# A gated mix of windowed attention and SwiGLU: how the first tokens, the identity and the warm-up are started

## The chip, the cores and the metric

The kernel runs on one core of one Trainium2 chip. The metric is the device time of one execution in microseconds (us); the figure for a kernel is the median of several runs. The core has five engines that run side by side, each with its own instruction stream: TensorE (PE: matrix products and transposes; its weight loads, PEld, overlap the products), VectorE (DVE), ScalarE (ACT), GpSimd (POOL) and SyncE (SP, which here only issues transfers). Transfers between memory and the on-chip buffers are issued by SyncE, ScalarE and GpSimd. Engines wait for each other and for transfers by semaphores.

## What is computed

```python
x = A_x                                    # 1 x 2048 x 512, bf16
g = _sigmoid((x * gate_w).sum(-1, keepdims=True))
a = _A_ref(x, A_wqkv, A_wo)                # attention: 32 heads of 16, causal, window of 256, output projection
b = _B_ref(x, B_w1, B_w3, B_w2)            # SwiGLU: (silu(x @ w1) * (x @ w3)) @ w2, inner width 1376
return g * a + (1 - g) * b
```

Every product contracts over the 512 features, so the kernel needs x with features on the partitions. The first 512 tokens are loaded as they lie and transposed on TensorE with an identity matrix; the later tokens come in through transposing transfers.

## The kernel before

All loads are issued at the start, most of them on SyncE's queue:

```python
def x_dma(t, h):                           # 256 tokens
    xs = xp.tile([P, 2, D], BF16, name=f"xs{h}")[:]
    nc.sync.dma_start(
        out=xs,
        in_=x2d[512 * t + 256 * h:512 * t + 256 * (h + 1), :].rearrange("(m p) d -> p m d", p=P))
    xs_tiles[2 * t + h] = xs

def x_dma1(j):                             # 128 tokens: j = 0 on SyncE's queue, j = 1 on ScalarE's
    if j == 0:
        xs_tiles[0] = xp.tile([P, 2, D], BF16, name="xs0")[:]
    (nc.scalar if j else nc.sync).dma_start(out=xs_tiles[0][:, j, :], in_=x2d[j * P:(j + 1) * P, :])
# [...]
nc.scalar.activation(out=scr[:, 1:2], in_=scr[:, 0:1], func=ACT.Tanh)
dma("x00", "SP", 3.5, lambda: x_dma1(0))                                 # tokens 0 to 127
dma("x01", "SP", 3.6, lambda: x_dma1(1))                                 # tokens 128 to 255
dma("x1", "SP", 4.5, lambda: x_dma(0, 1))                                # tokens 256 to 511
dma("k0", "ACT", 4.8, lambda: w_dma(nc.scalar, wk_sb, A_wqkv, 0, P, D))  # key weights, 128 columns
dma("q0", "SP", 5.8, lambda: w_dma(nc.sync, wq_sb, A_wqkv, 0, P))        # query weights, 128 columns
# [... more key and query weights, value weights, later tokens, feed-forward weights ...]
```

The numbers are the landing times that the kernel's own list scheduler assumes. This scheduler runs while the program is built: it gives every engine a fixed order of instructions, which doesn't depend on anything at run time.

GpSimd makes the identity (`ident`), the mask that separates even from odd heads (`eo`), columns of ones in the value tiles (they make the softmax denominators) and the triangular masks (`keep`), and issues the load of the gate vector:

```python
nc.gpsimd.memset(ident[:], 0.0)
nc.gpsimd.affine_select(out=ident[:], in_=ident[:], pattern=[[-1, P]],
                        compare_op=ALU.not_equal, fill=1.0, base=0, channel_multiplier=1)
nc.gpsimd.memset(eo[:], 1.0)
# [... two selects on eo, two operations on VectorE ...]
nc.gpsimd.memset(Vn[:, :, DH:2 * VW:DH + 1], 1.0)      # line 191
nc.gpsimd.memset(Vn[:, :, 2 * VW:], 1.0)
nc.gpsimd.memset(Vs[:, :, VW:], 1.0)
# [... keep: two memsets, four selects ...]
gate_dma()                                             # 128 x 512, broadcast, on GpSimd's queue
```

In the compiled program GpSimd's order is: fill of `ident`, fill of `eo`, the long fill of `Vn`, and only then the select that finishes `ident`.

TensorE begins with six products of constants that nobody reads (the warm-up), in the PSUM bank that the first transposes take next:

```python
b = ps.tile([P, 512], F32, name="g0")
for i in range(NWARM):                                 # NWARM = 6
    nc.tensor.matmul(b[:], lhsT=nc.const_aps.tensor(1.0, (P, P), BF16),
                     rhs=nc.const_aps.tensor(1.0, (P, 512), BF16), start=(i == 0), stop=(i == NWARM - 1))
```

Then come sixteen transposes of 128 x 128 in four groups (the groups `g_151` and `g_156` from tokens 0 to 255, `g_162` and `g_168` from tokens 256 to 511), their copies to `xT` on ScalarE and VectorE, and the first projections, keys (`g_176`, which needs the key weights) and queries (`g_182`), in halves of 256 tokens:

```python
for c in range(NDC):                                   # group of 128 tokens, `half` is 0 or 1
    nc.tensor.transpose(out=tx[:, c, :], in_=xs_tiles[0][:, half, c * P:(c + 1) * P], identity=ident[:])
# [...]
nc.tensor.matmul(b[:, 0:n], lhsT=(wq_sb if is_q else wk_sb)[:, dc, c * P:(c + 1) * P],
                 rhs=xT[:, dc, t0:t1], start=(dc == 0), stop=(dc == NDC - 1))
```

At the end, each tile of 128 tokens is written out from VectorE's result, for tiles 0 to 5 in two halves:

```python
for i in range(0, n, n // (2 if m < 6 else 1)):
    j = i + n // (2 if m < 6 else 1)
    nc.sync.dma_start(out=out2d[m * P:(m + 1) * P, n0 + i:n0 + j], in_=ot[:, i:j])
```

Of the kernel before, what the change touches and what calls it, by code (L numbers as in the profile page):

```python
# [9 lines left out]
BF16 = mybir.dt.bfloat16  # L10
# [3 lines left out]
DH = 16  # L14
WIN = 256
P = 128
# [3 lines left out]
VW = NPAIR * (DH + 1)  # L20

@with_exitstack
def kernel(
# [12 lines left out]
    nc = tc.nc  # L36
    x2d = A_x.flatten_outer_dims()
    out2d = out.flatten_outer_dims()
    S, D = x2d.shape
# [14 lines left out]
    Vn = pp.tile([P, NT, 2 * VW + DH], BF16, name="Vn")  # L54
    Vs = pp.tile([P, NT, VW + DH], BF16, name="Vs")
# [36 lines left out]
    def hold(pool, key, n):  # L92

        refs[(pool, key)] = n
# [10 lines left out]
    xs_tiles = {}  # L105

    def x_dma(t, h):
        xs = xp.tile([P, 2, D], BF16, name=f"xs{h}")[:]
        nc.sync.dma_start(
            out=xs,  # L110
            in_=x2d[512 * t + 256 * h:512 * t + 256 * (h + 1), :].rearrange("(m p) d -> p m d", p=P))
        xs_tiles[2 * t + h] = xs

    def x_dma1(j):
        if j == 0:
            xs_tiles[0] = xp.tile([P, 2, D], BF16, name="xs0")[:]
        (nc.scalar if j else nc.sync).dma_start(out=xs_tiles[0][:, j, :], in_=x2d[j * P:(j + 1) * P, :])

    def xt_dma(t, c):
        nc.sync.dma_start_transpose(out=xT[:, c, 512 * t:512 * (t + 1)],  # L120
# [10 lines left out]
    def dma(name, eng, at, fn):  # L131

        fn()
        land[name] = at

    nc.scalar.activation(out=scr[:, 1:2], in_=scr[:, 0:1], func=ACT.Tanh)
    dma("x00", "SP", 3.5, lambda: x_dma1(0))
    dma("x01", "SP", 3.6, lambda: x_dma1(1))
    dma("x1", "SP", 4.5, lambda: x_dma(0, 1))
    dma("k0", "ACT", 4.8, lambda: w_dma(nc.scalar, wk_sb, A_wqkv, 0, P, D))  # L140
    dma("q0", "SP", 5.8, lambda: w_dma(nc.sync, wq_sb, A_wqkv, 0, P))
# [15 lines left out]
                          in_=B_w2[0:(NFC - 1) * P, :].rearrange("(f p) n -> p f n", p=P)),  # L157
# [7 lines left out]
    def gate_dma():  # L165
        nc.gpsimd.dma_start(out=gw, in_=gate_w.rearrange("(x d) -> x d", x=1).to_broadcast([P, D]))

    def xn_dma():
        nc.sync.dma_start(out=xm[:], in_=x2d[S // 4:S // 2, :].rearrange("(m p) d -> p m d", p=P))
        nc.sync.dma_start(out=xn, in_=x2d[S // 2:S, :].rearrange("(m p) d -> p m d", p=P))  # L170

    def wo_dma():
        for j in range(2):
            wo_t.append(xp.tile([P, 2, D], BF16, name=f"xs{j}"))
            nc.sync.dma_start(out=wo_t[j][:], in_=A_wo[256 * j:256 * (j + 1), :].rearrange(
                "(c p) n -> p c n", p=P))
# [11 lines left out]
    nc.vector.tensor_reduce(out=maskEO[:, 0, 0, :], in_=eo[:], axis=mybir.AxisListType.X, op=ALU.add)  # L188
    nc.vector.tensor_scalar(out=maskEO[:, 0, 1, :], in0=maskEO[:, 0, 0, :], scalar1=-1.0, scalar2=1.0,
                            op0=ALU.mult, op1=ALU.add)  # L190
    nc.gpsimd.memset(Vn[:, :, DH:2 * VW:DH + 1], 1.0)
    nc.gpsimd.memset(Vn[:, :, 2 * VW:], 1.0)
    nc.gpsimd.memset(Vs[:, :, VW:], 1.0)

    keep = []
    for far in (False, True):
# [5 lines left out]
                                    base=-1 if far else 0, channel_multiplier=1 if far else -1)  # L202
        keep.append(k)
    gate_dma()

    class Load:
        def __init__(self, at):
# [6 lines left out]
    def pe_unit(dur, parts, deps, acq=(), rel=(), kind="", more=None):  # L214


        prev = None
        n = len(parts)
        more = more or [[]] * n
        for j, fn in enumerate(parts):  # L220
            o = Op("PE", dur / n, fn, deps + more[j] if j == 0 else [prev] + more[j], acq=acq if j == 0 else (),
                   rel=rel if j == n - 1 else (), kind=kind)
            o.cont = j > 0
            o.head = head = o if j == 0 else head
            prev = o
        return head, prev

    def bank(key, dtype=F32, shape=(P, 512)):
        n = slot("g", key)
        g_tile[key] = ps.tile(list(shape), dtype, name=f"g{n}")  # L230
        return g_tile[key]
# [367 lines left out]
    def add_out(m, n0=0, n1=512):  # L599
        key = ("o", m, n0)  # L600
        hold("g", key, 1)
        n = n1 - n0

        def pe(c0):
            def fn():
                b = bank(key) if c0 == 0 else g_tile[key]
                for c in range(c0, c0 + 1):
                    nc.tensor.matmul(b[:, 0:n], lhsT=OT[:, c * S + m * P:c * S + (m + 1) * P],  # L608
                                     rhs=wo_t[c // 2][:, c % 2, n0:n1], start=(c == 0),
                                     stop=(c == NDC - 1))  # L610
            return fn

        def fin(eng):
            ot = smpool.tile([P, D], BF16, name="ot")
            nc.vector.scalar_tensor_tensor(out=ot[:, 0:n], in0=g_tile[key][:, 0:n],
                                           scalar=gq[:, m:m + 1], in1=bsb[:, m, n0:n1],
                                           op0=ALU.mult, op1=ALU.add)
            for i in range(0, n, n // (2 if m < 6 else 1)):
                j = i + n // (2 if m < 6 else 1)
                nc.sync.dma_start(out=out2d[m * P:(m + 1) * P, n0 + i:n0 + j], in_=ot[:, i:j])  # L620

        a0, a = pe_unit(0.87 * n / 512, [pe(i) for i in range(NDC)], [pv_out[(c, m)] for c in range(NDC)] + [loads["wo"], down_pe[m]],
                        acq=[("g", key)], kind="out")
        Op("DVE", 0.05 + 0.65 * n / 512, fin, [a, down_op[m]], rel=[("g", key)], rank=0.2)
        return a0
# [203 lines left out]
    T0, PACE, NWARM = 11.2, 2.59, 6  # L829
# [200 lines left out]
    with tc.manual_schedule():  # L1030
        b = ps.tile([P, 512], F32, name="g0")
        for i in range(NWARM):
            nc.tensor.matmul(b[:], lhsT=nc.const_aps.tensor(1.0, (P, P), BF16),  # L1033
                             rhs=nc.const_aps.tensor(1.0, (P, 512), BF16), start=(i == 0), stop=(i == NWARM - 1))
        done = set()
        for o in order:
            if not wo_t and o in burst_ops[7:] and done.issuperset(z_op[0:4]):
                wo_dma()
                xn_dma()
            done.add(o)  # L1040
            if o.eng == "PE":
                o.fn()
            else:
                o.fn(o.eng)
# [27 lines left out]
```

The softmax here doesn't subtract the row's maximum and nothing guards it: scores larger than these inputs give would overflow.

## Time and profile before

| What | Value |
|---|---|
| median of three runs | 230.66 us (230.55 to 232.02) |
| the profiled run | 230.98 us, span of the core 229.3 us |
| PE / DVE / ACT / POOL busy | 225.5 / 180.6 / 175.5 / 175.3 us |
| long fill of `Vn` (line 191) | 0.98 to 3.25 us |
| first transpose on PE | 3.71 us |
| first projection on PE (`g_176`) | 5.38 us |
| last product ends | 226.49 us |

The profile is a record of one execution. Its summary gives the busy time of each engine as a share of the span; the chain of waits goes back from the last instruction to whatever released it; the timeline lists instructions by their start; the list of transfers gives the time from issue to landing. "PEld" is the weight load of TensorE. A name such as `g_151` is a PSUM tile, `xs_89` holds tokens 0 to 255, `xs_92` tokens 256 to 511, `on` is the identity and `OT` takes the gate vector in the beginning. Names such as `L191` are lines of the program. The granted clock that the profile lists is 1.00 in every stretch, also in the first microseconds, where the spacing of the products shows half the later rate.

### The profile page before, as it was taken

How to read it: one execution, taken by the hardware profiler on the slowest of the kernel's cores; microseconds unless marked ns; L12 is line 12 of the kernel's file. 1: busy time of each engine (PE TensorE's matmuls, PEld its weight loads, DVE VectorE, ACT ScalarE, POOL GpSimd, SP SyncE). 2: the span in 40 equal slices, each digit the busy share in tenths (PEclk: the TensorE clock that was granted, in tenths of full speed). 3: DMA queues.
4: the chain of work that ended last, by engine and by line, in shares of the span. 5: the costliest groups of instructions: out<-in, count | busy, mean ns of one | idle time of the engine just before them, and what ended most of it. 6: DMA issues, size and time to landing. Idle time of an engine off the chain costs nothing.

```text
span 229.3 us, 7274 instructions
## 1 busy us (share of the span) xinstructions
PE 225.5 (98%) x3060; PEld 102.1 (45%) x3060; DVE 180.6 (79%) x315; ACT 175.5 (77%) x144; POOL 175.3 (76%) x395
## 2 busy tenths in 40 slices
PE   8999999999999999999999999999999999999995
PEld 4543433535344443544353435444443444354544
DVE  2768599999998997879758596949987688876754
ACT  3478889788989989787989897987899877977030
POOL 8048898888899898888878887877888878777200
PEclk9999999999999999999999999999999999999999
DMA  6999999401100000000000000000000001220202
GB/s 187 214 265 202 319 258 350 132 0 26 27 3 3 3 0 0 3 4 4 0 3 0 3 3 3 0 3 4 0 3 1 3 4 37 70 82 0 94 3 93
DMA packets 20337, 13.81 MB, mean 60 GB/s; under 512 B 9680, under 2 KB 20016, under 8 KB 20304
## 3 DMA queue, kind: packets, MB, share of 16 engines
q1 hardware_dynamic: 19056, 11.80, 18.3%
q0 software_dynamic: 432, 1.25, 3.4%
q8 instruction: 24, 0.39, 0.7%
q10 hardware_dynamic: 816, 0.30, 0.5%
q14 instruction: 9, 0.07, 0.1%
HBM read 8.55 MB, written 2.10 MB: 46 GB/s over the span
## 4 chain that ended last, share of the span: by engine, by line
PE 97%; POOL 1%; issue 0%; DVE 0%; POOLq 0%
PE big L710 11%; PE g_1928 L578 1%; PE g_3349 L578 1%; PE g_2556 L578 1%; PE g_2293 L578 1%; PE g_3614 L578 1%; PE g_1297 L578 1%; PE g_4322 L578 1%; PE g_4387 L578 1%; PE g_3016 L578 1%; PE g_3813 L578 1%; PE g_2168 L578 1%; PE g_4282 L578 1%; PE g_2755 L578 1%; PE g_1650 L578 1%; PE g_4503 L578 1%
## 5 line engine op out<-in xcount | busy, mean ns | idle before, releaser
L480 PEld LDWEIGHTS <-w_sb 128*128 128x128 bf16 x320 | 29.2, 98 | 35.3 <-issue 3.4
L784 PEld LDWEIGHTS <-Vn 64*32 64x32 bf16 x720 | 15.1, 91 | 2.9 <-issue 1.3
L784 PEld LDWEIGHTS <-Vs 64*32 64x32 bf16 x720 | 15.2, 91 | 0.2
L809 DVE STREAM_TRANSPOSE OT<-on 128x512 bf16<-128x512 bf16 x16 | 11.2, 703 | 0.1
L339 PEld LDWEIGHTS <-wk_sb 128*128 128x128 bf16 x68 | 6.2, 100 | 7.1 <-issue 1.5
L386 PEld LDWEIGHTS <-xT 128*128 128x128 bf16 x64 | 5.7, 98 | 7.4 <-issue 1.6
L339 PEld LDWEIGHTS <-wq_sb 128*128 128x128 bf16 x68 | 6.0, 98 | 6.7 <-issue 1.5
L410 POOL DMA_DIRECT2D Vs<-Vn x4 | 2.5, 616 | 8.2 <-DVE xs_92 L422 8.2
L608 PEld LDWEIGHTS <-OT 128*128 128x128 bf16 x60 | 5.6, 98 | 6.8 <-issue 0.2
L578 PEld LDWEIGHTS <-hT_680 128*128 128x128 bf16 (+1 forms) x44 | 4.0, 98 | 5.1 <-issue 0.8
L578 PEld LDWEIGHTS <-hT_2291 128*128 128x128 bf16 (+1 forms) x44 | 4.0, 98 | 5.0 <-issue 0.6
L422 DVE SCALAR_TENSOR_TENSOR OT<-OT 128x512 bf16<-128x512 bf16 x8 | 5.9, 757 | 0.0
L578 PEld LDWEIGHTS <-hT_345 128*128 128x128 bf16 (+1 forms) x44 | 3.9, 98 | 4.3
L584 ACT ACTIVATE bsb<-g_4387,omg 128x512 bf16<-128x512 f32 x1 | 0.7, 687 | 6.2 <-PE g_4387 L578 6.2
L578 PEld LDWEIGHTS <-hT_3272 128*128 128x128 bf16 (+1 forms) x33 | 3.1, 98 | 3.8 <-issue 0.2
L734 POOL TENSOR_SCALAR_AFFINE_SELECT e_1530<-e_1530 64x256 bf16<-64x256 bf16 x6 | 3.7, 611 | 0.3
L734 POOL TENSOR_SCALAR_AFFINE_SELECT e_1261<-e_1261 64x256 bf16<-64x256 bf16 x6 | 3.6, 596 | 0.3
L734 POOL TENSOR_SCALAR_AFFINE_SELECT e_976<-e_976 64x256 bf16<-64x256 bf16 x6 | 3.2, 528 | 0.6 <-ACT e_976 L718 0.3
L1033 PE MATMUL g_144<-const-bfloat16-1.0 128*128 128x512 bf16 x6 | 2.7, 623 | 0.8 <-PEq L1056 0.8
L734 POOL TENSOR_SCALAR_AFFINE_SELECT e_423<-e_423 64x256 bf16<-64x256 bf16 x6 | 3.3, 542 | 0.3
L734 POOL TENSOR_SCALAR_AFFINE_SELECT e_3832<-e_3832 64x256 bf16<-64x256 bf16 x6 | 2.5, 411 | 1.1 <-ACT e_3832 L718 0.8
L734 POOL TENSOR_SCALAR_AFFINE_SELECT e_2774<-e_2774 64x256 bf16<-64x256 bf16 x6 | 2.5, 411 | 1.1 <-ACT e_2774 L718 0.8
(928 smaller groups left out, 853.9 us busy)
## 6 DMA issues: line engine op xcount, KB each, us to landing
w_sb<-in_B_w_dram SPq DMA_DIRECT2D x2, 864.0 KB, 8.0
w_sb<-in_B_w_dram SPq DMA_DIRECT2D x1, 1280.0 KB, 8.2
out_dram<-ot SPq DMA_DIRECT2D x9, 128.0 KB, 1.9
Vs<-Vn POOLq DMA_DIRECT2D x8, 136.0 KB, 4.1
w_sb<-in_B_w_dram SPq DMA_DIRECT2D x2, 512.0 KB, 4.9
OT<-in_A_x_dram SPq DMA_DIRECT2D x1, 1024.0 KB, 10.8
out_dram<-ot SPq DMA_DIRECT2D x13, 64.0 KB, 1.6
e_87<-in_A_wqkv_dram SPq DMA_DIRECT2D x1, 512.0 KB, 5.1
```

The costliest lines, as they stand in the source:

```text
L339: nc.tensor.matmul(b[:, 0:n], lhsT=(wq_sb if is_q else wk_sb)[:, dc, c * P:(c + 1) * P], rhs=xT[:, dc, t0:t1], start=(dc == 0), stop=(dc = ...
L386: nc.tensor.matmul(b[:], lhsT=xT[:, c, m * P:(m + 1) * P], rhs=wv_sb[:, c, :], start=(c == 0), stop=(c == NDC - 1))
L410: nc.gpsimd.dma_start(out=Vs[0:HK, ms, 0:VW], in_=Vn[HK:P, ms, 0:VW])
L422: nc.vector.scalar_tensor_tensor(out=x, in0=x, scalar=1.0, in1=gw, op0=ALU.mult, op1=ALU.mult, accum_out=zt[:, m:m + 1])
L480: nc.tensor.matmul(b[:], lhsT=wsb[:, dc, f * P:(f + 1) * P], rhs=xT[:, dc, t * 512:(t + 1) * 512], start=(dc == 0), stop=(dc == NDC - 1))
L578: nc.tensor.matmul(b[:], lhsT=h_tile[t][0:fs, f, (m % 4) * P:(m % 4 + 1) * P], rhs=w2_sb[0:fs, f, :], start=(f == 0), stop=(f == NFC - 1))
L608: nc.tensor.matmul(b[:, 0:n], lhsT=OT[:, c * S + m * P:c * S + (m + 1) * P], rhs=wo_t[c // 2][:, c % 2, n0:n1], start=(c == 0), stop=(c == ...
L710: nc.tensor.matmul(big[:, u, col:col + q1 - q0], lhsT=kt[32 * u:32 * u + 32, (j % 8) * P:(j % 8 + 1) * P], rhs=qt[32 * u:32 * u + 32, q0 - ...
L734: nc.gpsimd.affine_select(out=tri, in_=tri, pattern=[[0, 4], [-1 if far else 1, HK]], compare_op=ALU.is_ge, fill=0.0, base=-1 if far else ...
L784: nc.tensor.matmul(pv[i][32 * u:32 * u + 32, a - qa:b - qa], lhsT=v_of(j, i, 4 * c + u), rhs=e_tile[k][i * HK:i * HK + HK, u, col:col + b ...
L809: nc.vector.transpose(out=OT[:, c * S + qa:c * S + qb], in_=st["on"][:, 0:nb].rearrange("p b i d -> p (b i d)"))
L1033: nc.tensor.matmul(b[:], lhsT=nc.const_aps.tensor(1.0, (P, P), BF16), rhs=nc.const_aps.tensor(1.0, (P, 512), BF16), start=(i == 0), stop=( ...
```

## The change

The change is meant to let the first transposes start earlier. Tokens 0 to 127 are cut into two half rows of 256 features, one on each hardware queue. Tokens 128 to 255 move to SyncE's queue, tokens 256 to 511 to ScalarE's, ahead of the key weights there. On GpSimd the ones in the value tiles come last, after the identity, the masks and the gate's load. The warm-up products get 480 columns instead of 512. One output tile (tile 5) is written in one piece instead of two. The order of instructions on TensorE and VectorE, and that of ScalarE's computations, stay as they were.

```diff
@@ x_dma, x_dma1
-        nc.sync.dma_start(
+        nc.scalar.dma_start(
             out=xs,
             in_=x2d[512 * t + 256 * h:512 * t + 256 * (h + 1), :].rearrange("(m p) d -> p m d", p=P))
@@
-        (nc.scalar if j else nc.sync).dma_start(out=xs_tiles[0][:, j, :], in_=x2d[j * P:(j + 1) * P, :])
+            nc.scalar.dma_start(out=xs_tiles[0][:, 0, D // 2:D], in_=x2d[0:P, D // 2:D])
+            nc.sync.dma_start(out=xs_tiles[0][:, 0, 0:D // 2], in_=x2d[0:P, 0:D // 2])
+        else:
+            nc.sync.dma_start(out=xs_tiles[0][:, 1, :], in_=x2d[P:2 * P, :])
@@ the scheduler's assumed landing times
-    dma("x00", "SP", 3.5, lambda: x_dma1(0))
-    dma("x01", "SP", 3.6, lambda: x_dma1(1))
+    dma("x00", "SP", 3.3, lambda: x_dma1(0))
+    dma("x01", "SP", 3.7, lambda: x_dma1(1))
@@ GpSimd
-    nc.gpsimd.memset(Vn[:, :, DH:2 * VW:DH + 1], 1.0)
-    nc.gpsimd.memset(Vn[:, :, 2 * VW:], 1.0)
-    nc.gpsimd.memset(Vs[:, :, VW:], 1.0)
 # [... keep masks ...]
     gate_dma()
+    nc.gpsimd.memset(Vn[:, :, DH:2 * VW:DH + 1], 1.0)
+    nc.gpsimd.memset(Vn[:, :, 2 * VW:], 1.0)
+    nc.gpsimd.memset(Vs[:, :, VW:], 1.0)
@@ output
-            for i in range(0, n, n // (2 if m < 6 else 1)):
-                j = i + n // (2 if m < 6 else 1)
+            for i in range(0, n, n // (2 if m < 5 else 1)):
+                j = i + n // (2 if m < 5 else 1)
@@ warm-up
-            nc.tensor.matmul(b[:], lhsT=nc.const_aps.tensor(1.0, (P, P), BF16),
-                             rhs=nc.const_aps.tensor(1.0, (P, 512), BF16), start=(i == 0), stop=(i == NWARM - 1))
+            nc.tensor.matmul(b[:, 0:480], lhsT=nc.const_aps.tensor(1.0, (P, P), BF16),
+                             rhs=nc.const_aps.tensor(1.0, (P, 480), BF16), start=(i == 0), stop=(i == NWARM - 1))
```

## The prediction

> **What bounds the kernel now.** I read four views in this order: the summary of engines, the chain that ended last, the timeline of the first microseconds, and the list of transfers with their times to landing. The first two say where a change could count at all.
>
> ```profile
> PE 225.5 (98%) x3060; PEld 102.1 (45%) x3060; DVE 180.6 (79%) x315; ACT 175.5 (77%) x144; POOL 175.3 (76%) x395
> PE 97%; POOL 1%; issue 0%; DVE 0%; POOLq 0%
> ```
>
> The matrix engine is busy 98% of the span and makes 97% of the chain. The stretches of the span show it busy for all but about 0.03 us between 3.7 and 226.5 us. So what starts later than 3.7 us moves the end only if it makes this engine wait, and time can be saved only in the first 3.7 us, plus at the very end (2.8 us), which the change leaves alone. The chain, in order of time, names what fills that start:
>
> ```profile
> 0.95 0.10 POOL eo L183
> 1.05 2.22 POOL Vn L191
> 3.27 0.07 issue
> 3.33 0.30 POOL on L181
> 3.64 0.08 issue
> 3.71 0.58 PE g_151 L246 x4
> ...
> 5.58 0.66 PE g_176 L339 x4
> 6.24 0.44 PE g_182 L339 x4
> ```
>
> Columns are start, length, what. GpSimd fills the value tile with ones for 2.22 us (line 191) before it can finish the identity (line 181), at 3.63; the first transposes begin at 3.71. But the chain names only the last of several arrivals. The timeline and the transfers give the other two:
>
> ```profile
> 0.85 2.72 PE L1033 MATMUL g_144<-const-bfloat16-1.0 128*128 128x512 bf16 x6 [0.85 <-PEq L1056]
> 3.68 0.77 PEld L246 LDWEIGHTS <-xs_89 128*128 128x128 bf16 x8 [1.03 <-DMA xs_89<-in_A_x_dram]
> xs_89<-in_A_x_dram SPq DMA_DIRECT2D x1, 128.0 KB, 2.7
> xs_92<-in_A_x_dram SPq DMA_DIRECT2D x1, 256.0 KB, 3.1
> wk_sb<-in_A_wqkv_dram ACTq DMA_DIRECT2D x1, 128.0 KB, 3.5
> OT<-in_gate_w_dram POOLq DMA_DIRECT2D x1, 128.0 KB, 5.0
> ```
>
> The warm-up matmuls end at 0.85 + 2.72 = 3.57; the first transpose waits for them too, because it takes the same PSUM bank (its queue shows a semaphore wait that ends at 3.6). The first 128 tokens were issued at 0.81 and landed 2.7 later, at 3.51. So three things end within 0.12 us: tokens 3.51, warm-up 3.57, identity 3.63. **Taking away any one of them alone gains next to nothing**; the change touches all three.
>
> [...] four groups of 128 columns take 0.43 us (transposes up to 5.58), while 4 x 256 columns take 0.44 from 6.24 on, twice the rate; the group between, 0.66, holds the step, near 5.8. [...] In the trace the rate is 348 to 357 GB/s between 2.4 and 3.2 us, where 1 KB pieces move, and 287 between 4.0 and 4.8, where 256 B pieces do. [...]
>
> **The change part by part.**
> 1. *Identity first.* What stands before it then are four short fills: they overlap, and in the trace start about 0.1 apart, so that the last ends near 1.2. With 0.07 of wait and 0.29 for the select, the identity is ready near 1.6 instead of 3.63. It stops mattering. The fills of ones end later, near 6.8 (keep masks 2 x 0.55, the gate's issue 0.69, then 2.27 + 0.31 + 0.30), but the first value write starts at 10.18: hidden.
> 2. *Narrower warm-up.* Six matmuls lose 32 columns each. Weight loads start 0.427 apart for 512 columns, so 0.83 ns a column: 6 x 32 x 0.83 = 0.16 us. The end moves from 3.57 to 3.41.
> 3. *Two half rows.* Before, the first 128 KB shared the engines with the next 128 KB, issued at the same moment on the other queue, so 256 KB had to move for either to be done. Now both queues carry the first 128 KB. At 350 GB/s the 128 KB left out are 0.37 us. As the first 0.4 us of traffic is slow (166 GB/s) and half rows are small, I take 0.15 to 0.35: landing at 3.15 to 3.35.
>
> So the start is now set by the warm-up: 3.41 plus the same 0.14 from its end to the first transpose, 3.55 instead of 3.71. **The start gains 0.16 us, not the 2 us of the fill.**
> 4. *What comes behind.* Tokens 128 to 255 are issued at about 1.26 instead of 0.81 and have to be there at 3.71 + 0.43 - 0.16 = 3.98. 384 KB must have moved by then; before, this many had moved by about 3.4 (traffic summed over 0.2 us windows), so with some 0.45 from the last packet to the landing (tokens 256 to 511: last packets near 3.95, landed at 4.36), 3.85: just in time. Tokens 256 to 511 are issued at the same 1.26, now on ScalarE's queue; before they landed at 1.26 + 3.1 = 4.36 against a use at 4.42. The use is now at 4.26. The key weights no longer share the engines with them; the query weights do, 0.4 later. Estimate 4.15 to 4.35: up to 0.1 of wait.
> 5. *Key weights.* They were second on ScalarE's queue (issued 1.30, landed 4.8) and are now third (near 1.73), behind 256 KB. By their end 768 KB of tokens, key and query weights have moved, where before it was some 690 (summed in the same way to 4.4 us, where their last packets are); at 287 GB/s that is 0.28 us later, and what the next weights on SyncE's queue take adds up to 0.3. Landing 5.1 to 5.4; the use at 5.30 moves to 5.14. Expected wait 0.1.
> 6. *Output in one piece for tile 5.* One issue of 0.37 us less on SyncE's queue, near 200 us. No engine waits for it: 0.
>
> Sum: 0.16 gained, about 0.1 given back at the keys, 0.06 left. If the clock still steps up at 5.8, what moved ahead of it ran at half rate and is worth half: 0.03. If nothing has to wait, 0.16. So 0.03 to 0.16, around 0.1.
>
> **The rivals.**
> *The key weights become the wait.* For: five transfers in a row before them on two queues, and small pieces. Against: before they had 0.5 us of slack. If they land at 5.6, the first projection starts 0.3 later than before and the whole is 0.1 to 0.3 slower, near 230.9.
> *The gate vector disturbs.* Its transfer of 128 KB now leaves GpSimd near 3.2 instead of 4.54, so its packets come near 5.5 to 7 instead of 7 to 8.8, amid the value weights. They would delay these by 0.37; they landed at 3.32 + 5.1 = 8.4 and the first use is at 9.12. Against an effect: slack of 0.7, of which the earlier start takes 0.16. Worth 0.
> *The tokens set the start after all.* If half rows land no earlier than 3.51, the start is about 3.65, a gain of 0.06 or less, 230.6.
> *The clock step moves.* [...] each microsecond of half rate costs half a microsecond. The three times before, 230.55 to 232.02, spread by 1.5 us, much more than the whole effect. For: nothing else in a chain of 97% matrix work varies so easily. It makes the comparison uncertain, not the mean.
>
> **Range and chances.** The median of 230.66 less 0.1 is 230.56; as the change trims all three arrivals and some waits may turn out shorter than I sized them, I put 230.5. The range has to hold the spread between runs more than the effect: 229.9 to 231.2. 2% would be 4.6 us, more than the whole start of 3.7 us, so faster by that much is out of reach, and a slowdown of this size would need a wait of which I see no sign: 0.01 each way, 0.98 within.
>
> **What would show it.** In the changed kernel's profile: the ones-fill leaves the chain, and the warm-up or a transfer takes its place; identity done near 1.6; warm-up end near 3.41; first transpose at 3.5 to 3.6; the first weight load of the keys near 5.2, with an idle gap of about 0.1 ahead of it, ended by the transfer of key weights; the step of rate near 5.8; from there the same spacing as before, down to the end. I am wrong if the first transpose starts before 3.4 (the warm-up isn't the floor), if the keys start later than 5.4, or if the end moves by much more or less than the matrix engine's first warm group does.

## The result and the profile after

The changed kernel takes **232.25 us** (median of six runs, 231.67 to 233.34) against 230.75 us for the kernel before (six runs, 230.55 to 232.02). The ratio is 1.0064, 95% interval 1.0034 to 1.0093: 1.5 us slower, within 2%, and outside the predicted range of 229.9 to 231.2. The two profiled executions took 231.67 and 230.98 us, with spans of 230.0 and 229.3.

The summary of engines and the chain by engine of the changed kernel, which answer to the first two lines shown of before:

```profile
PE 225.8 (98%) x3060; PEld 102.0 (44%) x3060; DVE 180.8 (79%) x315; ACT 175.4 (76%) x144; POOL 174.6 (76%) x395
PE 93%; DMA 3%; ACT 1%; SPq 1%; POOL 0%; issue 0%; DVE 0%
```

The work of the matrix engine is the same. But 3% of the chain, which before was 97% matrix work, is now one transfer. The chain in order of time says which:

```profile
2.69 0.04 issue
2.73 0.51 SPq L127
3.24 0.04 issue
3.29 6.33 DMA e_87<-in_A_wqkv_dram
9.62 0.05 issue
9.66 1.04 PE g_215 L389 x4
```

Columns are start, length, what. `e_87` holds the value weights, 512 KB. They are issued at 3.29, land at 9.62, and the first value product starts 0.04 later. Before, it started at 9.12 and waited for no transfer. The lines of the timeline before, for the gate's load, the keys and the values:

```profile
4.54 0.69 POOL L166 DMA_DIRECT2D OT<-in_gate_w_dram  x1
5.38 0.87 PE L339 MATMUL g_176<-xT,wk_sb 128*128 128x256 bf16 x4
9.12 1.03 PE L386 MATMUL g_214<-e_87,xT 128*128 128x512 bf16 x4
```

The timeline of the changed kernel's first ten microseconds shows that what was meant to happen at the start did happen, and where the time went:

```profile
0.84 2.56 PE L1036 MATMUL g_145<-const-bfloat16-1.0 128*128 128x480 bf16 x6 [0.84 <-PEq L1059]
1.29 0.29 POOL L184 TENSOR_SCALAR_AFFINE_SELECT on<-on 128x128 bf16<-128x128 bf16 x1
2.92 0.69 POOL L169 DMA_DIRECT2D OT<-in_gate_w_dram  x1
3.52 0.77 PEld L249 LDWEIGHTS <-xs_89 128*128 128x128 bf16 x8 [0.97 <-DMA xs_89<-in_A_x_dram]
3.55 0.58 PE L249 MATMUL g_152<-on,xs_89 128*128 128x128 bf16 x4
4.45 0.77 PEld L264 LDWEIGHTS <-xs_93 128*128 128x128 bf16 x8 [0.15 <-DMA xs_93<-in_A_x_dram]
5.38 0.56 PEld L342 LDWEIGHTS <-wk_sb 128*128 128x128 bf16 x4 [0.16 <-DMA wk_sb<-in_A_wqkv_dram]
8.24 0.59 PEld L342 LDWEIGHTS <-wq_sb 128*128 128x128 bf16 x4 [0.28 <-DMA wq_sb<-in_A_wqkv_dram]
9.66 1.04 PE L389 MATMUL g_215<-e_87,xT 128*128 128x512 bf16 x4 [0.34 <-DMA e_87<-in_A_wqkv_dram]
```

Brackets hold the idle time before an instruction and what ended it. The identity is ready at 1.58 and the transposes start at 3.55, 0.16 earlier. At the keys, 5.38, nothing of this is left: two short waits for transfers (0.15, 0.16) have used it up. Then the later query weights are waited for (0.28), and the value weights (0.34 at the product, more at its weight load). None of these waits is in the profile before.

The list of transfers (issuing queue, size, microseconds from issue to landing) shows that it is the later transfers that became slow:

```profile
e_87<-in_A_wqkv_dram SPq DMA_DIRECT2D x1, 512.0 KB, 6.3
wq_sb<-in_A_wqkv_dram SPq DMA_DIRECT2D x2, 128.0 KB, 4.3
wk_sb<-in_A_wqkv_dram ACTq DMA_DIRECT2D x1, 128.0 KB, 3.6
OT<-in_gate_w_dram POOLq DMA_DIRECT2D x1, 128.0 KB, 5.1
```

Before, the first two were

```profile
e_87<-in_A_wqkv_dram SPq DMA_DIRECT2D x1, 512.0 KB, 5.1
wq_sb<-in_A_wqkv_dram SPq DMA_DIRECT2D x2, 128.0 KB, 3.6
```

and the others 3.5 and 5.0. The line of the query weights is the median of two transfers; the later one took 5.5 us (2.73 to 8.20) instead of 3.7. The key weights on ScalarE's queue (third line) are hardly slower. The change made that transfer third in its queue instead of second, but the delay is not there. The slow transfers are those under way together with the gate vector, which GpSimd now issues at 2.92 instead of 4.54; whether it is the cause, the experiments have to tell.

### The profile page after: what moved, and what is told of

It is laid out like the page before. It is cut to its first block, busy times and chain, and to the rows that moved or that the text cites. A ratio compares the mean times of both kernels' runs of the same rounds, so it can differ in the third digit from the quotient of the medians.

```text
span 230.0 us, 7275 instructions
## 1 busy us (share of the span) xinstructions
PE 225.8 (98%) x3060; PEld 102.0 (44%) x3060; DVE 180.8 (79%) x315; ACT 175.4 (76%) x144; POOL 174.6 (76%) x395
## 3 DMA queue, kind: packets, MB, share of 16 engines
q1 hardware_dynamic: 18784, 11.60, 18.4%
## 4 chain that ended last, share of the span: by engine, by line
PE 93%; DMA 3%; ACT 1%; SPq 1%; POOL 0%; issue 0%; DVE 0%
PE big L713 11%; DMA e_87<-in_A_wqkv_dram 3%; PE g_3615 L581 1%; PE g_1929 L581 1%; PE g_3350 L581 1%; PE g_2557 L581 1%; PE g_2294 L581 1%; PE g_4322 L581 1%; PE g_1298 L581 1%; PE g_4387 L581 1%; PE g_3017 L581 1%; PE g_2169 L581 1%; PE g_3814 L581 1%; PE g_2756 L581 1%; PE g_1651 L581 1%; PE g_4282 L581 1%
## 5 line engine op out<-in xcount | busy, mean ns | idle before, releaser
L1036 PE MATMUL g_145<-const-bfloat16-1.0 128*128 128x480 bf16 x6 | 2.6, 599 | 0.8 <-PEq L1059 0.8
```

What stands on the lines that cost most here:

```text
L1036: nc.tensor.matmul(b[:, 0:480], lhsT=nc.const_aps.tensor(1.0, (P, P), BF16), rhs=nc.const_aps.tensor(1.0, (P, 480), BF16), start=(i == 0), ...
```

## The experiments

All are compared with the kernel before on the same chip (230.81 to 230.87 us in each set). "Value weights" is the landing in the profiled execution of that kernel; one execution per kernel was profiled, the medians are of several. A piece is what one partition of the gate's tile gets.

| run | what it is | value weights land | median, us | ratio, 95% interval |
|---|---|---|---|---|
| before | the kernel before | 8.43 | 230.81 to 230.87 | 1 |
| after_again | the changed kernel | 9.95 | 232.33 | 1.0071, 1.0052 to 1.0090 |
| e1_gate_late | changed, gate issued at 4.33 | 8.41 | 231.19 | 1.0012, 1.0002 to 1.0022 |
| e2_pool_only | before, with the GpSimd order alone | 9.73 | 231.68 | 1.0034, 1.0021 to 1.0046 |
| e3_loads_only | before, with the token loads alone | 8.16 | 231.89 | 1.0044, 1.0029 to 1.0058 |
| e4_gate_rows | changed, gate read from 128 rows | 9.53 | 231.41 | 1.0022, 1.0014 to 1.0029 |
| e8_gate_scalar | changed, gate on ScalarE's queue at 2.93 | 9.82 | 231.86 | 1.0043, 1.0030 to 1.0056 |
| e9_small_gate | changed, gate 128 pieces, 16 KB | 9.50 | 231.79 | 1.0036, 1.0023 to 1.0050 |
| e10_gate_behind | changed, gate behind the value weights | 8.96 | 231.21 | 1.0011, 1.0002 to 1.0020 |
| e12_no_gate | changed, no gate transfer | 8.14 | 231.15 | 1.0011, 1.0002 to 1.0019 |
| e13_32_rows | changed, gate 32 pieces, 32 KB | 8.58 | 231.41 | 1.0028, 1.0014 to 1.0043 |
| e14_one_row | changed, gate one row, 1 KB | 8.09 | 231.17 | 1.0020, 1.0011 to 1.0029 |
| e5_loads_piece | e3 with tile 5 in one piece | 8.48 | 231.28 | 1.0019, 1.0007 to 1.0030 |
| e6_after_halves | changed, tile 5 in halves | 10.00 | 233.26 | 1.0102, 1.0088 to 1.0117 |
| e7_old_loads | before, with the identity first, gate late, short warm-up | 8.26 | 230.83 | 1.0006, 0.9993 to 1.0018 |
| e11_warm_only | before, with the short warm-up alone | 8.86 | 230.84 | 0.9997, 0.9987 to 1.0006 |

### Which part costs the time: the gate's load later, each part alone

The changed kernel again with the gate issued at about its old moment; then before with one part each.

```diff
# e1_gate_late: the changed kernel, GpSimd
-    gate_dma()
-    nc.gpsimd.memset(Vn[:, :, DH:2 * VW:DH + 1], 1.0)
     nc.gpsimd.memset(Vn[:, :, 2 * VW:], 1.0)
     nc.gpsimd.memset(Vs[:, :, VW:], 1.0)
+    nc.gpsimd.memset(Vn[:, 0:NT // 2, DH:2 * VW:DH + 1], 1.0)
+    gate_dma()
+    nc.gpsimd.memset(Vn[:, NT // 2:NT, DH:2 * VW:DH + 1], 1.0)
# e2_pool_only: before + the change's GpSimd order only
# e3_loads_only: before + the change's token loads (x_dma, x_dma1, assumed landings) only
```

> The changed kernel, with only the gate's load put back to about 4.65 us, where it was before (half of the ones-fill goes ahead of it). Theory G, the early gate transfer slows the value weights: they land at 8.4 to 8.7 instead of 9.6, the first value product starts near 9.1, the time is 230.5 to 230.9. Theory L, the new order and the half rows of the token loads push everything behind them: value weights still at 9.4 or later, time near 232.2.

> The kernel before, with only GpSimd's new order (so the gate's load leaves 1.6 us earlier). Theory G: value weights land about 1 us later than before, 9.3 or later, time 231.5 to 232.3. Theory L: nothing behind the loads changes, value weights at 8.4, time 230.7.

> The kernel before, with only the new token loads (half rows, other queues). Theory G: value weights at 8.4 to 8.6, the first projection up to 0.1 later than 5.38 because the key weights land near 5.3, time 230.7 to 230.9. Theory L: value weights near 9.5, time 231.8 to 232.3.

With the gate's load issued late, the changed kernel takes 231.19, above the expected 230.5 to 230.9, but 1.1 us less than with the early gate. Its list of transfers shows the value weights as fast as before:

```profile
e<-in_A_wqkv_dram SPq DMA_DIRECT2D x1, 512.0 KB, 5.1
```

and its timeline the first value product at 8.96, waiting for nothing:

```profile
8.10 1.03 PE L343 MATMUL g<-xT,wq_sb 128*128 128x512 bf16 x4
8.96 2.54 PE L390 MATMUL g<-e,xT 128*128 128x512 bf16 x10
```

The GpSimd order alone, with the old loads, brings the wait. In its list of waits (us in total, times, longest) these two are TensorE's weight load and product for the values, and its list of transfers has the slow landing:

```profile
PEld L386 <- DMA e<-in_A_wqkv_dram: 1.4, 1, 1.4
PE g L386 <- DMA e<-in_A_wqkv_dram: 0.9, 1, 0.9
```

```profile
e<-in_A_wqkv_dram SPq DMA_DIRECT2D x1, 512.0 KB, 6.4
wq_sb<-in_A_wqkv_dram SPq DMA_DIRECT2D x2, 128.0 KB, 4.3
OT<-in_gate_w_dram POOLq DMA_DIRECT2D x1, 128.0 KB, 5.5
```

So moving the ones behind the gate's load is what delays the value weights: making the identity early is harmless, but everything behind the old fill came forward by 1.6 us with it, the gate's load too. The loads alone were slower as well, which I had not expected, by 1.0 us, though their value weights landed early (8.16). Their loss is somewhere else, and the experiments on the output below find it.

### The changed kernel once more

> The changed kernel as it is, once more, on the same chip as the next three. If the early gate transfer (theory G) is the larger part: value weights at 9.5 or later, time 0.8 to 1.5 us above the kernel before on this chip, with a wider spread than the version with a later gate had (230.9 to 231.9).

It came out at 232.33, as the first time. Its profile is a worse draw of the same kind: the later query weights were issued at about 2.73 and landed at 8.52, the value weights at 9.95, and the first value product started at 10.00.

### What about the gate's transfer does it

It has 128 pieces that all read the same 1 KB, goes through GpSimd's own queue and moves 128 KB. Each of these could be the reason.

```diff
# e4_gate_rows: 128 different rows of x instead of one row 128 times (the gate's numbers change)
-        nc.gpsimd.dma_start(out=gw, in_=gate_w.rearrange("(x d) -> x d", x=1).to_broadcast([P, D]))
+        nc.gpsimd.dma_start(out=gw, in_=x2d[S // 2:S // 2 + P, :])
# e8_gate_scalar: nc.scalar.dma_start; tile 4 of the output in one piece too, so that
#                 the number of transfers on the hardware queues stays
# e9_small_gate: 64 of the 512 columns (the rest of the gate vector is left out, set to 0)
+        nc.gpsimd.dma_start(out=gw[:, 0:64], in_=gate_w[0:64].rearrange("(x d) -> x d", x=1).to_broadcast([P, 64]))
+        nc.gpsimd.memset(gw[:, 64:D], 0.0)
# e10_gate_behind: nc.sync.dma_start right behind the value weights; tile 4 as in e8
```

> The changed kernel, but the gate's transfer of the same size, queue and moment reads 128 different rows of x instead of one row 128 times (the gate is then computed from other numbers). If reading one row over and over is what makes that transfer slow and obstructive: value weights land by 8.9, time 230.6 to 231.0. If any transfer of 128 KB on GpSimd's queue at that moment does it: 9.5 and 232.2.

> The changed kernel, with the gate's transfer issued at about 3.0 us on ScalarE's hardware queue instead of 2.92 on GpSimd's (one more output tile in one piece keeps the number of hardware transfers). Theory G1, it is the software queue that holds some of the 16 engines: value weights at 8.9 or earlier, time 231.0 to 231.3. Theory G2, any further 128 KB at that moment: the first key and query weights come later still or the value weights land near 9.5, time 231.8 or more.

> The changed kernel, loading only 64 of the gate's 512 columns at the same moment (16 KB instead of 128 KB; the other columns are filled with zeros, so the gate is computed from 64 features only). If the delay goes with the bytes: value weights back at 8.4 to 8.7, time 231.0 to 231.3. If it goes with the number of pieces (128 as before) or with the mere presence of the queue: still above 9.3, time above 231.8.

> The changed kernel, with the gate's load right behind the value weights on SyncE's queue (one more output tile in one piece keeps the number of hardware transfers). Theory G, what counts is that the gate's transfer stays behind the weights: value weights at 8.2 to 8.6, time 230.9 to 231.2. It could be slower if the transposing loads behind it come late: tokens from 512 on are needed near 12.9 and landed at 10.9 before.

In the profiled executions neither other rows (9.53), nor another queue (9.82), nor an eighth of the bytes (9.50) brings the value weights back. Standing behind them instead of ahead does most of it: 8.96 and 231.21. That leaves the number of pieces, or the mere presence of a transfer ahead. Three runs separate these. All set the rest of the gate tile, or all of it, to zero, so that the gate is 0.5 where the vector is left out.

```diff
# e12_no_gate: no transfer
+        nc.gpsimd.memset(gw[:, :], 0.0)
# e13_32_rows: 32 pieces of 1 KB
+        nc.gpsimd.dma_start(out=gw[0:32, :], in_=gate_w.rearrange("(x d) -> x d", x=1).to_broadcast([32, D]))
# e14_one_row: one row of 1 KB, into a tile that nothing reads
+        nc.gpsimd.dma_start(out=grow, in_=gate_w.rearrange("(x d) -> x d", x=1))
```

> The changed kernel without the gate's transfer: GpSimd sets the gate tile to zero instead (0.3 to 0.6 us more of GpSimd before the ones; the gate is then 0.5 for every token, so the output isn't the reference's). All else, the loads too, is as in the changed kernel. If the gate's transfer, issued ahead of the value weights, is what delays them, these land at 8.3 to 8.6 instead of 9.62, the first value product starts at 8.9 to 9.4, as in the run with the late gate, and the time is 230.9 to 231.3. If the changed order on GpSimd or the loads delay the value weights by another way, they land later than 9.2 and the time stays above 231.7.

> The changed kernel with the gate's transfer cut to 32 of the 128 partitions (32 KB in 32 pieces of 1 KB; the other partitions are set to zero, so the gate is 0.5 there). Issued at the same 2.92. If the engine time of the gate's packets is what counts, a quarter of it remains (0.2 of 0.84 us per engine), and the value weights land at 8.6 to 8.9, time 231.2 to 231.5. If a single held engine is enough to hold up all, as the run with an eighth of the bytes in 128 pieces suggests (value weights at 9.50), they still land at 9.3 or later and the time stays at 231.7 or above.

> The changed kernel with the gate's transfer cut to a single row of 1 KB into one partition of a tile that nothing reads; the gate tile is set to zero. Issued at the same 2.92. If it is the mere presence of a transfer on GpSimd's queue ahead of the value weights that holds engines up, the value weights still land later than 9.2. If it is what its packets occupy, they land at 8.3 to 8.7, as without any gate transfer, and the time is 230.9 to 231.3.

The transfer lists of the three, in this order, the value weights:

```profile
e<-in_A_wqkv_dram SPq DMA_DIRECT2D x1, 512.0 KB, 4.8
```

```profile
e<-in_A_wqkv_dram SPq DMA_DIRECT2D x1, 512.0 KB, 5.3
```

```profile
e<-in_A_wqkv_dram SPq DMA_DIRECT2D x1, 512.0 KB, 4.8
```

A single row costs nothing (8.09 against 8.14 with none; the trace has it as sixteen packets of 64 bytes), so the mere presence of a transfer isn't it, and the changed order on GpSimd without the gate's transfer does no harm. With 128 pieces ahead the value weights land 1.36 us later than with none when these carry 16 KB, and 1.39 to 1.86 later in the five profiled executions with the new loads where they carry 128 KB. So bytes don't order these landings. The number of packets doesn't either: e9, e13 and e14 all have sixteen, of 1 KB, 2 KB and 64 bytes. What is left of the three is the number of pieces. With 32 of them the landing is 0.44 us later, but this isn't shown to be a delay: the nine other executions without 128 pieces ahead lie between 8.09 and 8.96, the seven with them between 9.50 and 10.00. Nothing was run between 32 and 128 pieces.

The times are less clear-cut than these landings. Taken against the kernel before on the same chip, and with the 0.32 us of e12_no_gate off, the gate's transfer costs 1.2 us in the changed kernel, 0.7 on ScalarE's queue, 0.6 with 16 KB, 0.3 with 32 pieces, 0.2 with 128 different rows and nothing with one row. So it isn't ruled out that reading one row again and again, or the bytes, has a part in the time. One profiled landing can be far from the usual one: the profiled execution of e4_gate_rows took 231.65 us, and 16 of its 22 executions were faster.

(The times of e13 and e14 can't be read from their profiled executions: these have the value product at 9.63 and 9.57 with the weights there since 8.58 and 8.09. Their last weight loads at the slow rate are at 6.54 and 6.49; in e12_no_gate, with the product at 9.02, that is at 5.00.)

### What is held up: the sixteen reports of a transfer

The end of a transfer comes in the trace as sixteen reports, as many as the profile counts DMA engines. That each of them is one engine's end of its share is my reading: the trace doesn't say which engine reports. The later query weights, in us from the start, from the trace:

```
before: 5.50 5.52 5.64 5.69 5.77 5.79 5.80 5.82 5.96 6.02 6.06 6.17 6.36 6.39 6.46 6.51
after:  5.84 6.09 6.14 6.14 6.21 6.25 6.26 6.70 6.86 7.20 7.27 7.28 7.74 8.15 8.16 8.20
```

Five reports are in by 6.21, where before twelve were; nine come later than the last one did before (6.51), and the last three 1.7 us later, at 8.15 to 8.20. The weight load that waits for this transfer starts at 8.24, so this wait lasted until the latest of the sixteen.

The value weights come behind these in the same queue. The trace has them as 512 packets of 1 KB, of 0.047 us each. If sixteen engines share them evenly, one after another, that is 32 x 0.047 = 1.5 us: an estimate of 6.51 + 1.5 = 8.0 for the slowest engine in the kernel before, where they landed at 8.43, and of 8.20 + 1.5 = 9.7 in the changed one, where they landed at 9.62. In the seventeen profiled executions they landed 1.4 to 2.6 us after the last of the query weights. So the chain seems to be: with the gate's pieces ahead, some of the sixteen shares of the query weights end late, and the value weights are late behind them, by 1.19 us where the query weights were late by 1.69. That the gate's pieces hold up some of the engines, and the same ones in both transfers, is argued from these times and not shown. The value weights' own sixteen reports come within 0.1 us of each other, before (8.36 to 8.43) as after (9.52 to 9.62). Nor does it look like the slowest engine alone: half of the value weights' packets had ended by 6.54 before and by 7.73 after, the last at 8.06 and 9.22.

How slow the gate's pieces are is in the profile, as the time that the queue's packets took between 5 and 9.4 us, in shares of sixteen engines. Before:

```profile
q0 software_dynamic: 48, 0.13, 18.4%
```

after:

```profile
q0 software_dynamic: 48, 0.13, 19.2%
```

and with an eighth of the bytes (e9_small_gate):

```profile
q0 software_dynamic: 32, 0.02, 5.1%
```

Columns are packets, MB, share. 18.4% of 4.4 us is 0.81 us per engine, 19.2% is 0.84. This is the same before and after, and more than twice the 0.37 that I had got from bytes over rate: the 32 packets of 4 KB took 0.42 us each on the average, from 0.16 up to 1.03 (before: 0.40, from 0.16 up to 1.18), where 1 KB of value weights took 0.05. **That the gate's packets are slow beside other traffic was there to read in the profile before.** But this is no engine time that others lose, since packets overlap (in e4_gate_rows SyncE's queue alone has 121.4% in the same stretch), and it doesn't tell the size of the delay: with shares of 19.2, 10.2 (e4_gate_rows) and 5.1% the value weights landed at 9.62, 9.53 and 9.50. In e9_small_gate fifteen reports of the query weights were in by 6.46 and the last came at 7.85; one packet of 1 KB on SyncE's queue took 1.53 us. Why single packets take so long there, the trace doesn't show.

### The output in one piece, and the end

The loads alone (e3_loads_only) have their last VectorE instruction at 226.82, as early as before (226.86), and yet a span 0.8 us longer. The time from there to the end is 3.30 us, not 2.42. SyncE's waits between 225 and 232 us in e3_loads_only:

```profile
SPq L675 <- DVE ot L671: 1.2, 2, 0.6
SPq L1070 <- DMA out_dram<-ot: 1.0, 1, 1.0
SPq L1070 <- PEq L1070: 0.7, 2, 0.5
```

In the kernel before the same list has the first and third of these, under its own line numbers, and not the middle one:

```profile
SPq L672 <- DVE ot L668: 1.2, 2, 0.6
SPq L1067 <- PEq L1067: 0.7, 2, 0.5
```

At the end of the program SyncE waits for one semaphore after another. When these waits end, in us, from the traces:

```
before: 227.28 227.36 227.43 227.50 227.57 228.03 228.11 228.18 228.36
e3:     227.24 228.31 228.38 228.45 228.52 228.99 229.07 229.14 229.21
```

The last output lands at about 228.3 in both. Before, its semaphore is the last in the list, and the others are done by then. In e3 it is the second, and the seven behind it, each 0.07 us and one 0.47, are only then gone through. In these traces the transfers of SyncE's and ScalarE's queues (56 before, 57 in e3) take eight completion semaphores over and over. The loads alone add one transfer, so that the last output gets the next semaphore of the eight. The change takes one transfer away again by writing tile 5 in one piece. Two runs test this, one in each direction.

```diff
# e5_loads_piece: e3_loads_only;   e6_after_halves: the changed kernel
-            for i in range(0, n, n // (2 if m < 6 else 1)):      # e5; in e6 m < 5 becomes m < 6
+            for i in range(0, n, n // (2 if m < 5 else 1)):
```

> The loads alone, plus tile 5 written in one piece, so that the number of transfers on the two hardware queues is that of the kernel before. Theory T, the tail: the loads alone added one transfer, the last output got the next completion semaphore in the rotation, and SyncE, which waits for these one after the other at the end, came to it as its second wait instead of its last. Then the tail after the last operation on VectorE goes from 3.3 us back to 2.4, and the time from 231.9 to 231.0. Rival, the piece costs or saves nothing: 231.9.

> The changed kernel with tile 5 still written in two halves. Theory T: its tail grows by 0.85 us, so 0.8 to 0.9 above the changed kernel on this chip. Rival (my own prediction, the piece is worth 0): the same as the changed kernel.

With the count restored the loads alone go from 231.89 to 231.28, and their stretch after the last VectorE instruction is 2.40 again; with tile 5 in halves the changed kernel goes from 232.33 to 233.26 (3.28). SyncE's waits at the end of e6_after_halves have the extra line, too:

```profile
SPq L1070 <- DMA out_dram<-ot: 1.0, 1, 1.0
```

So with the new loads, writing tile 5 in one piece saves 0.6 to 0.9 us, not by what it moves but by the semaphore that the last output gets.

### The rest: warm-up and GpSimd order without the new loads

```diff
# e7_old_loads: before + GpSimd's block of e1_gate_late + 480 columns in the warm-up
# e11_warm_only: before + 480 columns in the warm-up
-                             rhs=nc.const_aps.tensor(1.0, (P, 512), BF16), ...)
+                             rhs=nc.const_aps.tensor(1.0, (P, 480), BF16), ...)
```

> A candidate: identity first, gate's load at its old moment, narrower warm-up, but the token loads and the output as before. First transpose at 3.6, set by the tokens' landing near 3.53; keys at 5.3; value weights at 8.4; the unexplained 0.12 us near 176 us, which only kernels with the new loads showed, is gone. Time 230.7 to 230.8, at best 0.1 below the kernel before.

> The kernel before with only the narrower warm-up. My prediction's step: the identity (3.63) and the tokens (3.51) still hold the first transpose at 3.71, so nothing is gained: 230.7 to 230.9, within 0.1% of the kernel before. Rival: the warm-up was the real floor, first transpose at 3.55.

Both are where the kernel before is, 230.83 and 230.84. In e7 the first transpose is at 3.55 and the first value product at 9.25: a start 0.16 us earlier isn't worth anything that can be measured. In e11 the first transpose is at 3.67, held by the identity (3.62): the warm-up alone gives 0.04, as the prediction said of any one of the three. No run was faster than the kernel before by more than its interval.

## Why the prediction was wrong

**What bounds it, and the start (steps 1 to 3): right.** Identity at 1.58 (predicted near 1.6), end of the warm-up 0.84 + 2.56 = 3.40 (3.41), first transpose at 3.55 (3.55). The half rows landed at 2.83 and 2.99, earlier than the estimated 3.15 to 3.35, and it didn't matter, since the warm-up was the floor. That the first two loads of tokens were under way side by side is in the trace of the kernel before: between 2.4 and 2.6 us the packets of SyncE's queue took 47.6% of the time of sixteen engines and those of ScalarE's 54.3%. That each had to wait for the bytes of the other was an estimate.

**What comes behind (steps 4 and 5): right in kind, a little short.** Tokens 128 to 255 landed at 3.77 (3.85), tokens 256 to 511 at 4.41 (4.15 to 4.35), key weights at 5.34 (5.1 to 5.4). The keys started at 5.38 in one execution of the changed kernel and 5.48 in the other, past the 5.4 named as a sign of being wrong. So the 0.16 was given back entirely, where I had kept 0.06. With the gate late and the output's count kept, the kernel is still 0.3 us above before (231.19, and 231.15 without the gate's transfer), and the loads alone with the output's count kept are 0.5 above it (e5), while the old loads (e7) are not: the new loads cost 0.3 to 0.5 us instead of costing 0.1 of a gain of 0.16.

**"Worth 0", the rival of the gate vector: this is the step that failed.** The rival was stated with the right sign, the right transfer and the right slack: 128 KB among the value weights, landing at 8.4, first use at 9.12. The term that was mis-sized is the 0.37 us of delay, taken as bytes over rate. The value weights landed 9.62 - 8.43 = 1.19 us later, more than three times that. The slack of 0.7 took up the rest, which leaves 0.5: the product moved from 9.12 to 9.66. In the second execution it was 10.00 - 9.12 = 0.88. From here the changed kernel ran as before but for 0.14 us, so the delay went to the end. By the medians the early gate costs 232.33 - 231.19 = 1.1 us in the changed kernel (e1_gate_late), or 0.8 alone (e2_pool_only). A smaller slip stands beside it: I had the gate leave GpSimd "near 3.2"; it left at 2.92, ahead of the value weights at 3.29 and not at the same moment. In e1_gate_late and e10_gate_behind, with the gate behind them, the value weights land at 8.41 and 8.96.

**"No engine waits for it: 0", step 6: wrong too**, but without effect on the sum: taken with the new loads, the one piece only keeps the end as it was (2.41 us after the last VectorE instruction, 2.42 before). Without it the kernel is 0.9 us slower still (e6_after_halves). I had compared the durations of issues and had not counted transfers.

**The sum.** 1.1 us for the early gate and 0.3 to 0.5 for the new loads make the 1.5 that was measured. Of the second part 0.12 us is a longer stretch of matrix work between about 176 and 179 us that all kernels with the new loads have but e8_gate_scalar, and none with the old loads. I can't name its cause.

**The spread, and what the profiles don't show.** "The clock step moves" is right as far as the step of the rate goes: the last weight load at the slow rate (0.147 us before and 0.151 after, with 0.098 further on) is at 5.80 before, 5.78 and 4.15 in two executions of the changed kernel, and between 3.7 and 6.9 in the others. What sets its moment isn't shown. The profiled pair differs by 0.7 us and the medians by 1.5. In all seventeen profiled executions the time is the start of the first value product plus 221.9 to 222.1 us, or plus 222.9 where the last output's semaphore stands early (e3, e6). From this, as an estimate: the medians of 232.3 and 230.75 belong to first value products near 10.2 and 8.9. So the two profiled executions of the changed kernel, with 9.66 and 10.00 the fastest of their sets, have less of the wait than is usual, and no trace shows a usual one. I think that the step has a part in this: before, an early step lets the products run ahead until the value weights land at 8.4, and in the changed kernel they run into weights that aren't there until 9.6 to 10.0. It wasn't tried by itself. The same estimate puts the product of e4_gate_rows (median 231.41) near 9.3, so its value weights mostly land before the 9.53 of its profile; why 128 different rows cost less than one row read 128 times stays open.

## What to carry to other kernels

When an engine's list of work is reordered, follow each transfer it issues: here a load that moved ahead of others delayed them by far more than its bytes at the usual rate (1.19 us against 0.37), and the wait for the query weights lasted until the latest of sixteen reports (8.20, where five were in by 6.21). Packets that take long in the profile before (0.40 us for 4 KB, where 1 KB of value weights took 0.05) are a warning, though not a price. Where a broadcast of many pieces isn't needed early, place it behind the loads that something waits for (value weights at 8.96 in e10_gate_behind instead of 9.62). When a load is added or an output is split, compare the time from the last computation to the end too, since the order of the final waits changed it by 0.9 us here.

## What the runs showed of the hardware

- With 128 pieces issued 0.4 us ahead of it, a transfer of 512 KB landed at 9.50 (16 KB) and at 9.53 to 10.00 (128 KB), against 8.14 with none and 8.09 with a single row.
- One of the sixteen reports of a transfer came late by itself in e9_small_gate: fifteen of the query weights were in by 6.46, the last at 7.85. The transfer behind them landed at 9.50, where without the gate's transfer it landed at 8.14.
- The last waits of the program were gone through one after another, 0.07 us each and one 0.47. With the last output's semaphore last among them, the stretch after the last computation was 2.4 us, with it second 3.3.
- The step of the matrix engine's rate came between 3.7 and 6.9 us in executions of nearly the same start. The granted clock that the profile lists is 1.00 on both sides of it; the length of the weight loads shows it: mostly 0.147 to 0.152 us before the step and 0.098 after it.
